# A first entry's attention in two ranges of nine tiles, products by 64 keys, and an order from measured durations

## The chip, the cores and the metric

One core of a Trainium2 chip. The metric is the device time of one execution in microseconds; lower is better.

## The reference

Inputs are q, k, v of shape (8, 8, 576, 64) (entries, heads, tokens, head size) and two matrices w_in (512, 2048) and w_out (2048, 512), all fp32.

```python
scores = 0.125 * q @ k^T                   # per entry and head
allowed: 0 <= i - j < 32                   # heads 0 to 3
         0 <= i - j < 128, (i - j) % 4 == 0   # heads 4 to 7
attn = exp(scores - max) ; attn /= sum + 1e-9
x = (attn @ v), heads side by side         # (4608, 512)
h = x @ w_in ; out = (h * sigmoid(1.702 h)) @ w_out
```

The dilated heads are stored with their tokens sorted by remainder of 4, so that both kinds of head are a band of 32 positions.

## The kernel before

**Layout.** A pair is two heads of one entry: 32 pairs, four to an entry, two of them plain and two dilated. x is kept transposed, 512 features in four chunks of 128, and a pair fills one chunk. The first three entries are multiplied in the plain way (`Group`, hidden chunks f = 0 to 15, up and down projection); the other five and the leftover 64 tokens of every entry go in three blocks through products of sums of matrices (`Block`). The fp32 numbers of the projections are split into a high and a low fp32r part, and one product is three matmuls of 128x512 (high x high, low x high, high x low). Attention itself is in fp32; one of its matmuls is two passes in the trace.

**The weights** come as 64-bit numbers, 32 units (`wi0`, `wo0`, `wi1`, ...) of 128x512. `decode` makes the high and low part of each from eight steps: load into one of five cells, value and low word on ACT (L393, L394), the sign on ACT or DVE (L387, L389), a shift on DVE, a sum, a copy as high part, a subtraction as low part (L348, on DVE or POOL). Hidden chunk f needs `wi{f}` and then `wo{f}`.

**Attention of a pair** (`scores`, `softmax`, `product` or, for the first entry, `first_product`, then `drain_x`). A tile is 32 queries by 64 keys. For the first entry the 576 queries are four ranges of 144 in the four groups of 32 partitions, five tiles to a range and head, of which the last is half empty: 640 columns for two heads. A bias matmul writes the mask first (L470), the scores are added (L482), then maximum, difference, exponential, sum, sum + 1e-9, reciprocal, two multiplications (one half each, usually on POOL), two 32x32 transposes. `first_product` (L572) multiplies into four PSUM banks, one a range, and waits for all four (`FOUR`). Its drain is a high part on ACT and a low part on DVE, from PSUM to `xh` and `xl` in the tile `xs`. For later pairs the transposed attention is copied into `bt` (64 keys by 32 queries for each window), and `product` (L595) is nine windows x two ranges x two heads = 36 matmuls of 32 columns with stationary v of 64x64.

**The order.** `Plan` collects all operations with costs by engine, urgency and dependences; `ordered` places them one after the other on a modelled time line and writes them out in that order for each engine, so an engine executes strictly what the list says. Where TensorE would be idle in the first 60 us it inserts matmuls on `ident` (L1243) or small ones (L1247). Its numbers decide order only.

Of the kernel before, what the change touches and what calls it, by code (L numbers as in the profile page):

```python
# [27 lines left out]
AHEAD = 0.58  # L28
# [7 lines left out]
NW = 9  # L36
HALF = 32 * NW
ROW = S // 4
INNER = 24


PE, ACT, DVE, POOL, DMA = range(5)
LATER = {PE: 0.0, ACT: 0.0, DVE: 0.51, POOL: 0.04, DMA: 0.0}
LATENCY = {PE: 0.3, ACT: 0.2, DVE: 0.2, POOL: 0.2, DMA: 0.2}


class Plan:

# [5 lines left out]

# [14 lines left out]

# [20 lines left out]
    def ordered(self, warm, warm_until, soon):  # L103
        order, starts = self.placed(warm_until, soon)
        for _ in range(ROUNDS):
            order, starts = self.placed(warm_until, soon, self.latest(starts, SINCE))
        ops = self.ops
        return [(ops[i][2] if i is not None and i >= 0 else lambda e, i=i: warm(i), e) for i, e in order]

    def placed(self, warm_until, soon, late=None):  # L110


# [8 lines left out]
        free = [0.0] * 5  # L121
        port, bus = [0.0], [0.0]
        issued, blocks = [0], [0.0]

        def start(i, e):
            held = port[0] if e == POOL or (e == DVE and ops[i][0][e] < 0) else 0.0
            if e == DMA and ops[i][1][0] >= 2000.0 and ops[i][0][e] > 100:
                held = bus[0] - 3.0
            if e == DMA and late is not None and SINCE < ready[i][e] < late[i] - CALM and late[i] < 9.0e3:
                held = max(held, ready[i][e] + 1.2)  # L130
            return max(free[e], ready[i][e], held)

        def fetched(count, when, cost):

            n = issued[0]
            issued[0] += count
            for j in range(len(blocks) - 1, 1 << 30):
                edge = 193 + 256 * j
                if edge >= n + count or edge > 1500:
                    return when + cost  # L140
                part = cost * (edge - n) / count
                at = max(when + part, blocks[j])
                blocks.append(at + (6.1 if at < 18.0 else 4.2))
                when, cost, n, count = at, cost - part, edge, count - (edge - n)
# [7 lines left out]
        while any(open_):  # L152
# [29 lines left out]
            if e == PE and when < warm_until:  # L182

                at, size = max(free[e], 1.0), 0.26 if when > 8.0 else 0.44
                if when < SHORT and blocks[-1] < when - 0.3:

                    small = min((193 + 256 * (len(blocks) - 1) - issued[0]) // 4 + 1, int((when - at - 0.1) / 0.045))
                    order.extend([(None, e)] * small)
                    at = fetched(4 * small, at, small * 0.045)
# [3 lines left out]
            order.append((i, e))  # L193
            starts[i] = when
            if e == PE:
                cost = fetched(ops[i][5], when, cost) - when
            if e == POOL or (e == DVE and ops[i][0][e] < 0):
                port[0] = when + cost

            free[e] = when + (cost if e != DMA else 0.7 if cost < 100 else 0.43)  # L200
            if e == DMA:
                bus[0] = max(bus[0], when + 2.0) + cost / 360.0
                cost = bus[0] - when
            for j in users[i]:
                for to in ready[j]:
                    gap = 0.0 if to == e == PE else 0.13 if to == e else LATENCY[to]
                    ready[j][to] = max(ready[j][to], when + cost + gap + ops[j][4])
# [4 lines left out]
        return order, starts  # L212
# [3 lines left out]
def tile_windowed_attention_then_gated_mlp(  # L216
# [3 lines left out]
    vp: bass.AP,  # L220
    first_v: bass.AP,
# [13 lines left out]
    plan = Plan()  # L235
# [16 lines left out]
    wi_last = temp([P, NF - NSUM, 2, DM], F32R, "wi_last", "wi_last")  # L252
    wo_kept = fixed([P, NOUT, 2, DM], F32R, "wo_kept")
    wo_last = temp([P, NF - NOUT, 2, DM], F32R, "wo_last", "wo_last")
# [5 lines left out]

    bt = fixed([P, 2, 2, NW + 1, 32], F32, "bt")
    bt_all = bt.rearrange("p y a n w -> p (y a n w)")
    arena = fixed([P, NU, GT], F32, "arena")
# [3 lines left out]

    def wi(f):
        return wi_kept[:, f] if f < NSUM else wi_last[:, f - NSUM]

    def wo(f):
        return wo_kept[:, f] if f < NOUT else wo_last[:, f - NOUT]
# [10 lines left out]
    prs = [fixed([P, 2, QT, W], F32, f"pr{j}") for j in range(2)]  # L283
    mxs = [fixed([P, 2, QT], F32, f"mx{j}") for j in range(3)]
    sms = [fixed([P, 2, QT], F32, f"sm{j}") for j in range(3)]
# [4 lines left out]
    prs.append(third[:, 0:2 * QT * W].rearrange("p (a t w) -> p a t w", a=2, t=QT))  # L290
    cts.append(third[:, 2 * QT * W:4 * QT * W].rearrange("p (h a t q) -> p h a t q", h=2, a=2, t=QT))
# [13 lines left out]
    ones = fixed([P, 32], F32, "ones")  # L305
    V.memset(ones, 1.0)
# [7 lines left out]
    early = arena[:, 17]  # L314
    classes = early.bitcast(BF16)[:, 0:QT * W].rearrange("p (t w) -> p t w", t=QT)
    band = early.bitcast(BF16)[0:32, QT * W:QT * W + W]
# [5 lines left out]
    for j in range(4):  # L322
        V.tensor_copy(out=plain[32 * j:32 * j + 32], in_=band[:, None, :].broadcast_to([32, QT, W]))

    A.activation(classes, plain, AF.Copy)
    V.memset(classes[:, 0, 0:32], NEG)
    V.memset(plain[0:32, 0, 0:32], NEG)

    def mask_dilated():

        A.activation(mask, plain, AF.Copy)
# [966 lines left out]
```

## Time and profile before

| | us |
|---|---|
| median of 3 runs | 836.37 (835.21 to 836.68) |
| profiled execution | 835.02 |
| its span | 833.2 |
| PE busy in the span | 816.0 (98%) |
| DVE, ACT, POOL busy | 641.1, 519.3, 331.3 |
| granted TensorE clock, mean | 0.994 |

PE is TensorE, DVE VectorE, ACT ScalarE, POOL GpSimd, SP the queue that issues loads and stores. Busy time of PE counts matmuls that overlap their neighbours, so what matters there is where it is idle and how far apart matmuls start. Idle time of another engine costs nothing unless PE waits for it.

### The profile page before, as it was taken

Reading aid. Unit: us, or ns where it says so; the run is one execution under the profiler, and the core shown is the slowest. Engines: PE = TensorE matmul, PEld = TensorE weight load, DVE = VectorE, ACT = ScalarE, POOL = GpSimd, SP = SyncE. Lnnn points to the kernel's source line nnn. Section 1 sums busy time; section 2 is a strip of 40 time slices with the busy share of each in tenths; the row PEclk is TensorE's granted clock in tenths of the full one; section 3 lists DMA queues with packets and bytes.
Section 4 is the critical chain, followed back from the end, with each engine's and each line's share of the span. In section 5 each row is a group of like instructions: output and inputs, shape, how many; then the busy total and the mean of one; then the engine's idle time right before and its main releaser. Section 6 shows DMA issues by size and latency. Waiting matters only on the chain.

```text
span 833.2 us, 20312 instructions
## 1 busy us (share of the span) xinstructions
PE 816.0 (98%) x8024; PEld 661.3 (79%) x8024; DVE 641.1 (77%) x1041; ACT 519.3 (62%) x964; POOL 331.3 (40%) x299
## 2 busy tenths in 40 slices
PE   6899999999999999999999999999999999999998
PEld 4678878888887888877878877888888888888886
DVE  6897898788897878887988899856468956465566
ACT  7898896776586667677666665445436534544430
POOL 3344326465545355233364454441223615204230
PEclk9799999999999999999999999999999999999999
DMA  9476867898887655997677969676556667655635
GB/s 358 148 256 184 246 193 228 305 299 281 298 279 261 234 188 195 344 320 237 215 263 237 290 217 284 230 256 212 183 184 203 201 215 262 206 190 193 199 124 180
DMA packets 110894, 195.70 MB, mean 235 GB/s; under 512 B 27728, under 2 KB 56656, under 8 KB 110800
## 3 DMA queue, kind: packets, MB, share of 16 engines
q1 hardware_dynamic: 110656, 194.29, 70.5%
q8 instruction: 63, 1.03, 0.5%
q14 instruction: 31, 0.25, 0.1%
q10 hardware_dynamic: 144, 0.13, 0.0%
HBM read 147.98 MB, written 45.09 MB: 232 GB/s over the span
## 4 chain that ended last, share of the span: by engine, by line
PE 90%; DVE 5%; issue 1%; DMA 1%; ACT 1%; SPq 0%; DVEq 0%; ACTq 0%
PE hp_m L850 16%; PE up_r L993 9%; PE up_q L993 8%; PE up_p L993 8%; PE second_q_Q L1111 5%; PE acc_m L787 5%; PE second_r_Q L1111 5%; PE acc_m L788 5%; PE acc_m L791 5%; PE second_p_Q L1111 4%; PE av L595 3%; PE sp L482 3%; PE second_r_Z L1111 3%; PE second_R L1111 3%; PE second_q_Z L1111 3%; PE second_p_Z L1111 2%
## 5 line engine op out<-in xcount | busy, mean ns | idle before, releaser
L348 POOL TENSOR_TENSOR arena<-arena 128x256 f32<-128x256 f32 (+3 forms) x112 | 120.0, 1084 | 155.0 <-DVE arena L348 53.5
L850 PE MATMUL hp_m<-xs,wi_kept 128*128 128x512 f32 x504 | 130.1, 400 | 0.6 <-DVE xs L348 0.4
L850 PEld LDWEIGHTS hp_m<-xs,wi_kept 128*128 128x128 f32 x504 | 93.5, 189 | 21.7 <-DVE xs L348 0.9
L993 PE MATMUL up_r<-wi_kept,xs 128*128 128x512 f32 x336 | 88.7, 389 | 0.0
L993 PE MATMUL up_q<-wi_kept,xs 128*128 128x512 f32 x336 | 87.5, 389 | 0.5 <-DVE arena L348 0.5
L993 PE MATMUL up_p<-wi_kept,xs 128*128 128x512 f32 x336 | 84.8, 395 | 0.8 <-ACT arena L341 0.6
L348 DVE TENSOR_TENSOR wo_kept<-arena,wo_kept 128x512 fp32r<-128x512 f32 x89 | 71.3, 811 | 18.1 <-ACT wo_kept L341 17.7
L341 ACT ACTIVATE wo_kept<-arena 128x512 fp32r<-128x512 f32 x104 | 64.4, 627 | 33.4 <-PE second_r_Q L1111 8.7
L348 POOL TENSOR_TENSOR wo_kept<-arena,wo_kept 128x512 fp32r<-128x512 f32 x32 | 43.1, 1350 | 97.0 <-ACT wo_kept L341 86.4
L993 PEld LDWEIGHTS up_p<-wi_kept,xs 128*128 128x128 f32 x336 | 61.8, 188 | 16.4 <-ACT arena L341 1.6
L993 PEld LDWEIGHTS up_q<-wi_kept,xs 128*128 128x128 f32 x336 | 63.0, 188 | 13.9 <-DVE arena L348 0.9
L993 PEld LDWEIGHTS up_r<-wi_kept,xs 128*128 128x128 f32 x336 | 63.1, 188 | 13.1
L348 POOL TENSOR_TENSOR pr<-pr,sm 128x320 f32<-128x320 f32 x52 | 42.2, 829 | 62.2 <-DVE sm L512 50.5
L348 POOL TENSOR_TENSOR wo_kept<-wi_last_units,wo_kept 128x512 fp32r<-128x512 f32 x20 | 28.6, 1428 | 83.7 <-ACT wo_kept L341 58.0
L787 PE MATMUL acc_m<-gh,wo_kept 128*128 128x512 f32 x156 | 61.5, 394 | 0.0
L788 PE MATMUL acc_m<-gh,wo_kept 128*128 128x512 f32 x156 | 60.8, 390 | 0.0
L341 ACT ACTIVATE bt<-ct 32x320 f32<-32x320 f32 x121 | 56.8, 469 | 4.7 <-DVE ct L533 2.5
L348 DVE TENSOR_TENSOR gl<-arena,gh 128x512 fp32r<-128x512 f32 x47 | 41.2, 877 | 11.8 <-PE acc_m L791 5.8
L348 DVE TENSOR_TENSOR arena<-arena 128x512 f32<-128x512 f32 (+1 forms) x63 | 47.2, 757 | 3.9 <-ACT arena L1015 1.7
L1015 ACT ACTIVATE arena<-arena 128x512 f32<-128x512 f32 x40 | 25.1, 627 | 35.1 <-DVE arena L348 35.0
L341 ACT ACTIVATE wo_kept<-wi_last_units 128x512 fp32r<-128x512 f32 x46 | 28.8, 629 | 25.9 <-PE second_r_Z L1111 7.1
L858 ACT ACTIVATE arena<-hp_m 128x512 f32<-128x512 f32 x48 | 28.6, 597 | 25.2 <-PE hp_m L850 16.1
(260 smaller groups left out, 1868.4 us busy)
## 6 DMA issues: line engine op xcount, KB each, us to landing
xs<-sums SPq DMA_DIRECT2D x168, 256.0 KB, 3.3
out_weights<-sums_o SPq DMA_DIRECT2D x63, 512.0 KB, 3.9
qk<-qk_dram SPq DMA_DIRECT2D x29, 576.0 KB, 5.6
v<-vp_dram SPq DMA_DIRECT2D x28, 576.0 KB, 4.4
xs<-sums_o SPq DMA_DIRECT2D x21, 512.0 KB, 3.5
sums<-arena SPq DMA_DIRECT2D x32, 256.0 KB, 4.3
sums_o<-arena SPq DMA_DIRECT2D x32, 256.0 KB, 4.7
arena<-wi_dram SPq DMA_DIRECT2D x15, 512.0 KB, 4.7
```

The costliest lines, as they stand in the source:

```text
L341: A.activation(dst, src, AF.Copy, scale=scale)
L348: (V if e == DVE else G).tensor_tensor(out=dst, in0=a, in1=b, op=op)
L482: T.matmul(dst[:, w:w + n], u["qk"][rows, at:at + 32], u["qk"][rows, S + first:S + first + n], start=not masked(k), stop=True, tile_positi ...
L595: T.matmul(to[rows, 0:32], u["v"][keys, a, m], bt[keys, k % 2, a, m], start=True, stop=True, tile_position=(D * r, D * a), skip_group_chec ...
L787: T.matmul(self.acc[j], w[:, 0, cols], high, start=f == 0, stop=False)
L788: T.matmul(self.acc[j], w[:, 1, cols], high, start=False, stop=False)
L791: T.matmul(self.acc[j], w[:, 0, P * j:P * j + P], low, start=False, stop=f == NF - 1)
L850: T.matmul(hps[f], wi(f)[:, st, cols], mv[:, c], start=c == 0 and k == 0, stop=c == NC - 1 and k == 2)
L858: add({ACT: 0.60}, -10.0, lambda e: A.activation(g32, hps[f], AF.Tanh, scale=0.851), (place,), ("g32",))
L993: T.matmul(self.banks[place], xs[:, slot, at:at + P], wi_kept[:, 2 * a + c, mv], start=fresh and c == 0 and k == 0, stop=c == 1 and k == 2 ...
L1015: add({ACT: 0.60}, -10.0, lambda e: A.activation(unit(dst), src(), AF.Gelu_apprx_sigmoid), need, keys)
L1111: T.matmul(self.second[key], w[:, st, cols], mv, start=fresh and y == 0 and k == 0, stop=y == 1 and k == 2, skip_group_check=True)
```

## The change

**First entry.** Two ranges of 288 queries, nine tiles each; the four groups of 32 partitions are range and head, so a pair has 9 x 64 = 576 columns and 36 score matmuls, without the key ranges cut at the end. The masks of single tiles come from five bands (`first_masks`), by matmuls of 64 to 448 columns. The 1e-9 is a 65th column of each tile and goes into the sum, so the small addition is gone for all pairs. `first_product` uses two of the four banks, in turn; for the first two pairs (plain heads) v is loaded with zeros in the other head's 64 columns, so that one matmul of 64 keys and 128 columns serves both heads (19 instead of 46 matmuls); the dilated ones keep 64 columns (36 instead of 40). The inputs of the first entry go where the last weights will be decoded (`wo_last`, `wi_last`, the arena, the `qk` tile) and no weight's cell is taken from other tiles any more.

**Later pairs.** v is cut in blocks of 64 keys, six and four to the two ranges, 768 columns instead of 1152; a block meets 96 queries, so `bt` holds 64 keys by 96 queries with zeros in the corners (cleared once), and `product` is 20 blocks, two of them cut at a bank's end: 22 matmuls of 32 to 96 columns that add up in PSUM. Drains are cut accordingly.

**Order.** The planner has other costs, a model of late instruction blocks, of landing loads and of a lowered clock, and takes the best of its four rounds.

```diff
-NW = 9
-HALF = 32 * NW
+LOW = 8
+SPAN = W + 32
+NT = S // 64
+WIDE_QK, WIDE_V = (2, 2, 2, 2), (P, P, D, D)
+FIRST_QK, FIRST_V = (-9.0, -8.04, -4.96, -4.2), (-8.44, -6.17, -3.7, -3.23)
+EARLY = {0: 1.63, 1: 12.3, 2: 14.6, 3: 16.9}
+FIRST_W = {0: -8.22, 1: -7.65, 2: -5.03, 3: -4.69, 4: -2.5}
...
-    bt = fixed([P, 2, 2, NW + 1, 32], F32, "bt")
+    bt = fixed([P, 2, 2, QT, SPAN], F32, "bt")
...
-    ones = fixed([P, 32], F32, "ones")
-    V.memset(ones, 1.0)
+    ones = ident.bitcast(F32)[:, 0:32]
...
+    G.memset(bt[:, :, :, :, 0:W], 0.0)
...
+    def first_masks(k):
+        u = pairs[k]
+        sp = bank([P, 2, GT], "sp", f"sp_{k}").rearrange("p a n -> p (a n)")
+        u["all"] = sp[:, 0:NT * W].rearrange("p (t w) -> p t w", w=W)
+        spans = ((0, 1, 2), (1, 4, 0), (4, 5, 3), (5, 6, 4), (6, 8, 0), (8, 9, 0)) if dilated(k) else (
+            (0, 1, 1), (1, 8, 0), (8, 9, 0))
+        for t, to, n in spans:
+            T.matmul(sp[:, W * t:W * to], ident, bands[:, n:n + 1].broadcast_to([P, to - t, W]), start=t in (0, 8),
+                     stop=False, skip_group_check=True)
+
+    def first_scores(k):
...
+        for t in range(NT):
+            for r in range(2):
+                i = NT * r + t
+                keys = slice(at + 32 * i - 32, at + 32 * i + 32)
...
+                for a in range(2):
+                    rows, g = slice(D * a, D * a + D), 2 * r + a
+                    T.matmul(u["all"][32 * g:32 * g + 32, t], u["qk"][rows, 32 * i:32 * i + 32], u["qk"][rows, keys],
+                             start=False, stop=True, tile_position=(D * a, 32 * g), skip_group_check=True)
...
-    def inverse(k, urgency):
-        sm, SM = sms[turn(k)], f"sm{turn(k)}"
-        add({DVE: -0.15}, urgency, lambda e: V.tensor_scalar(
-            out=sm, in0=sm, scalar1=1.0e-9, scalar2=None, op0=ALU.add), (), (SM,))
...
+    def first_banks(k):
+        return f"acc{2 * (k % 2)}", f"acc{2 * (k % 2) + 1}"
...
+        for s in range(0 if dilated(k) else -1, NT):
+            for r in range(2):
+                if s < 0 and r == 0:
                     continue
...
+                for a in range(P // WIDE_V[k]):
+                    rows = slice(D * r, D * r + D) if WIDE_V[k] == P else slice(D * r + 32 * a, D * r + 32 * a + 32)
+                    T.matmul(u["x"][WIDE_V[k] * a:WIDE_V[k] * a + WIDE_V[k], r, at:at + n], u["v"][rows, s % (NT + 1)],
+                             ct[rows, first:first + n], start=begin, stop=s == NT - 1,
+                             tile_position=(rows.start, WIDE_V[k] * a), skip_group_check=True)
...
-        for m in range(NW):
+        pieces = [(r, a, m) for m in range(QT + 1) for r in range(2) for a in range(2) if r or 0 < m < QT]
+        begun = set()
+        for r, a, m in pieces:
+            rows, keys = slice(D * a, D * a + D), slice(D * r, D * r + D)
+            first, last, at = max(SPAN * m - W, 0), min(32 + SPAN * m, SPAN * QT if r else SPAN * QT - SPAN), max(W * m - W, 0)
...
+            for n, (to, at, first, last) in enumerate(parts):
+                if first < last:
+                    T.matmul(to[rows, at:at + last - first], u["v"][keys, a, m], bt_flat[keys, k % 2, a, first:last],
+                             start=(r, a, n) not in begun, stop=True, tile_position=(D * r, D * a), skip_group_check=True)
+                    begun.add((r, a, n))
```

How the order moves, at three places. On PE, before, the fourth pair's scores (`sp`) and the second pair's product (`first_x`) at 19 to 26 us stand like this:

```order
L482 MATMUL sp_439<-arena 32x64 x35
L482 MATMUL sp_439<-arena 32x48
L482 MATMUL sp_439<-arena 32x16
L482 MATMUL sp_439<-arena 32x64 x3
L572 MATMUL first_x<-ct_92,arena 64x32 x6
L572 MATMUL first_x<-ct_92,arena 64x64 x24
L572 MATMUL first_x<-ct_92,arena 64x48 x8
L572 MATMUL first_x<-ct_92,arena 64x16 x8
L850 MATMUL hp_m_0_556<-xs,wi_kept 128x512 x3
```

and now, the third pair's scores (`sp_312`) with the products of the first (`ct_84`) and second pair (`ct_85`), then masks and scores of the fourth (`sp_419`):

```order
L658 MATMUL first_x<-ct_84,first_135 128x64 x16
L658 MATMUL first_x<-ct_84,first_135 128x32 x2
L537 MATMUL sp_312<-arena 32x64 x36
L953 MATMUL hp_m_0_391<-xs,wi_kept 128x512 x3
L658 MATMUL first_x<-ct_85,arena 128x32
L658 MATMUL first_x<-ct_85,arena 128x64 x16
L658 MATMUL first_x<-ct_85,arena 128x32 x2
...
L517 MATMUL sp_419<-arena,ident 128x128
...
L537 MATMUL sp_419<-arena 32x64 x36
```

The second product has moved ahead of the fourth scores, and both are shorter.

On ACT, before, the last two drains (`xs<-first_x 128x4x128`) and the steps up to the first chunk's tanh (`hp_m_0`):

```order
L341 ACTIVATE xs<-first_x 128x4x128
L393 ACTIVATE arena<-arena 128x512 x2
L394 ACTIVATE arena<-arena 128x512 x2
L387 ACTIVATE arena<-arena 128x512
L341 ACTIVATE xs<-first_x 128x4x128
L394 ACTIVATE arena<-arena 128x512
L387 ACTIVATE arena<-arena 128x512
L393 ACTIVATE arena<-arena 128x512
L858 ACTIVATE arena<-hp_m_0_556 128x512
```

and now, from the six decoding steps ahead of the fourth exponential (`pr_82`) to the fourth drain (L432 is the value, L433 the low word, L426 the sign):

```order
L433 ACTIVATE arena<-arena 128x512
L426 ACTIVATE arena<-arena 128x512
L592 ACTIVATE pr_82<-pr_82 128x9x64
L383 ACTIVATE xs<-first_x 128x4x128
L383 ACTIVATE wo_kept<-arena 128x512
L433 ACTIVATE arena<-arena 128x512
L426 ACTIVATE arena<-arena 128x512
L432 ACTIVATE arena<-arena 128x512
L433 ACTIVATE arena<-arena 128x512
L432 ACTIVATE arena<-arena 128x512
L433 ACTIVATE arena<-arena 128x512
L383 ACTIVATE xs<-first_x 128x4x128
```

Seven steps stand between the last two drains instead of five, and the fourth exponential is right ahead of the third drain.

On SP, before, the first loads (`wi_dram` and `wo_dram` are weights):

```order
L427 DMA qk_126<-qk_dram 128x1152
L383 DMA arena<-wi_dram 128x512
L440 DMA v_129<-first_v_dram 128x768
L427 DMA arena<-qk_dram 128x1152
L383 DMA arena<-wo_dram 128x512
L427 DMA arena<-qk_dram 128x1152
L383 DMA arena<-wi_dram 128x512
L383 DMA bt<-wo_dram 128x512
L427 DMA arena<-qk_dram 128x1152
L440 DMA arena<-first_v_dram 128x768
```

and now (a weight is 524 KB, a load of 1152 columns 590 KB, one of 1280 columns 655 KB):

```order
L473 DMA first_135<-first_qk_dram 128x1152
L487 DMA first_135<-first_v_dram 128x1280
L422 DMA arena<-wi_dram 128x512
L473 DMA first_qk_139<-first_qk_dram 128x1152
L422 DMA arena<-wo_dram 128x512
L487 DMA arena<-first_v_dram 128x1280
L473 DMA arena<-first_qk_dram 128x1152 x2
L487 DMA first_v_199<-first_v_dram 128x576
L487 DMA arena<-first_v_dram 128x576
L422 DMA arena<-wi_dram 128x512
```

All inputs of the first entry now stand ahead of the third weight, where four weights stand between them in the rows of before.

## Rows read from the trace of the kernel before

**Rows 1.** Stretches: length, busy PE, PEld, DVE, ACT, POOL (instructions), granted clock, DMA, GB/s

```profile
0.00:20.00 20.00, 13.62 (x478) 8.49 (x479) 12.86 (x35) 15.30 (x22) 6.78 (x15) 1.00 0.91 356
20.00:25.00 5.00, 2.48 (x128) 2.25 (x127) 4.60 (x10) 4.88 (x7) 2.85 (x3) 0.63 0.49 188
...
40.00:130.00 90.00, 89.77 (x1064) 72.00 (x1063) 78.70 (x141) 80.93 (x141) 35.30 (x30) 1.00 0.69 217
42.00:829.00 787.00, 783.51 (x7174) 639.23 (x7172) 609.21 (x969) 484.67 (x914) 317.26 (x277) 1.00 0.71 234
```

**Rows 2.** Waits of PE: total us, times, longest

```profile
PE sp L482 <- issue: 3.8, 3, 2.0
...
PE first_x L572 <- issue: 1.2, 1, 1.2
```

**Rows 3.** Timeline of PE: start, length, line, shape, count, idle before

```profile
4.86 1.45 PE L482 MATMUL sp<-qk 64*32 64x64 f32 x84
...
15.27 0.38 PE L482 MATMUL sp<-arena 64*32 64x64 f32 x21 [1.67 <-issue]
15.58 1.50 PE L572 MATMUL first_x<-ct,v 32*64 32x32 f32 x92
...
19.28 0.32 PE L482 MATMUL sp<-arena 64*32 64x64 f32 x9
21.56 1.37 PE L482 MATMUL sp<-arena 64*32 64x64 f32 x75 [1.96 <-issue]
22.85 1.18 PE L572 MATMUL first_x<-ct,arena 32*64 32x32 f32 x53
25.21 0.91 PE L572 MATMUL first_x<-ct,arena 32*64 32x64 f32 x39 [1.18 <-issue]
...
34.29 1.08 PE L572 MATMUL first_x<-ct,arena 32*64 32x64 f32 x80
...
38.46 3.93 PE L850 MATMUL hp_m<-xs,wi_kept 128*128 128x512 f32 x16 [0.42 <-DVE xs L348]
42.23 0.39 PE L787 MATMUL acc_m<-gh,wo_kept 128*128 128x512 f32 x1
```

**Rows 4.** Timeline of ACT, DVE and POOL, first 46 us

```profile
5.64 0.67 ACT L393 ACTIVATE arena<-arena 128x512 f32<-128x512 f32 x1 [0.39 <-DMA arena<-wi_dram]
...
6.68 0.81 DVE L502 TENSOR_REDUCE mx<-sp 128x10 f32<-128x640 f32 x1
...
6.90 1.34 ACT L387 ACTIVATE arena<-arena 128x512 f16<-128x512 f32 x1
...
8.39 0.74 ACT L506 ACTIVATE pr<-pr 128x640 f32<-128x640 f32 x1
...
10.50 0.17 DVE L510 TENSOR_SCALAR sm<-sm 128x10 f32<-128x10 f32 x1
...
11.66 1.58 POOL L348 TENSOR_TENSOR pr<-pr,sm 128x320 f32<-128x320 f32 x2 [6.70 <-DVE sm L512]
...
35.41 1.08 ACT L341 ACTIVATE xs<-first_x 128x512 fp32r<-128x512 f32 x1 [0.49 <-PE first_x L572]
...
37.33 1.08 DVE L348 TENSOR_TENSOR xs<-first_x,xs 128x512 fp32r<-128x512 f32 x1
```

**Rows 5.** Timeline of all engines near 99 us

```profile
98.51 1.29 POOL L348 TENSOR_TENSOR wi_kept<-arena,wi_kept 128x512 fp32r<-128x512 f32 x1 [3.63 <-ACT wi_kept L341]
...
99.78 2.88 PE L850 MATMUL hp_m<-xs,wi_kept 128*128 128x512 f32 x12
```

**Rows 6.** Timeline of PE around one product and one scores

```profile
102.59 0.25 PE L595 MATMUL av<-bt,v 64*64 64x32 f32 x2
...
103.77 0.50 PE L787 MATMUL acc_m<-gh,wo_kept 128*128 128x512 f32 x1
...
108.07 0.97 PE L482 MATMUL sp<-qk 64*32 64x64 f32 x72
108.97 1.65 PE L850 MATMUL hp_m<-xs,wi_kept 128*128 128x512 f32 x6
```

More of the change, by code (lines that the diff above doesn't have):

```diff
@@ L27 @@
 NU = 22
-AHEAD = 0.58
+AHEAD = 0.62
 ROUNDS, SINCE, CALM, ROOM = 3, 130.0, 8.0, 2.5
@@ L103, in ordered @@
     def ordered(self, warm, warm_until, soon):
-        order, starts = self.placed(warm_until, soon)
-        for _ in range(ROUNDS):
-            order, starts = self.placed(warm_until, soon, self.latest(starts, SINCE))
+        best = None
+        late = None
+        for n in range(ROUNDS + 1):
+            order, starts, end = self.placed(warm_until, soon, late)
+            if best is None or end < best[1]:
+                best = order, end
+            late = self.latest(starts, SINCE)
+        self.ends.append(best[1])
         ops = self.ops
-        return [(ops[i][2] if i is not None and i >= 0 else lambda e, i=i: warm(i), e) for i, e in order]
+        return [(ops[i][2] if i is not None and i >= 0 else lambda e, i=i: warm(i), e) for i, e in best[0]]
+    ends = []
     def placed(self, warm_until, soon, late=None):
@@ L136, in fetched @@
             issued[0] += count
[L137 to L144, printed above, removed]
+            recent.append((n, when))
+            while True:
+                k = len(arrived) - 1
+                edge = FIRST_EDGE + BLOCK * k
+                if edge >= n + count:
+                    break
+                part = cost * max(0.0, edge - n) / count
+                at = max(when + part, arrived[k])
+                ahead = [t for m, t in recent if m >= edge - DECODED]
+                asked = max(arrived[k], min([at, *ahead]))
+                arrived.append(asked + (6.2 if asked < 18.0 else 4.4 if bus[0] > asked + 0.3 else 3.0))
+                when += at - when - part
+            del recent[:-60]
+            return when + cost
         open_ = [set() for _ in free]
@@ L211, in placed @@
                         open_[to].add(j)
-        return order, starts
+        return order, starts, free[PE]
 @with_exitstack
@@ L610, in drain_x @@
         if k >= INNER:
+            near = [(0, low, lambda first, last: u["x"][:, 0, first:last], True)]
+            far = (lambda first, last: u["x"][:, 1, first - low:last - low]), True
+        else:
+            near = [(0, ROOMY, lambda first, last: u["x"][:, 0, QT * W + first:QT * W + last], True),
+                    (ROOMY, low, lambda first, last: u["x"][:, 1, QT * W + first - ROOMY:QT * W + last - ROOMY], True)]
+            far = (lambda first, last: u["av"][:, first - low:last - low]), False
@@ L726, in attention @@
         places = ("sp",) if k >= INNER else ("left", "av", "sp") if joint else ("left", "av")
-        add({PE: 1.8 if joint else 0.85}, urgency - 1.0e5, work,
-            (lots(k)[1], *(f"bt{k % 2}.{m}" for m in range(8)), *need), places, 1.0)
+        add({PE: 2.26 if joint else 1.35}, urgency - 1.0e5, work,
+            (lots(k)[1], *(f"bt{k % 2}.{m}" for m in range(8)), *need), places, 0.0, count=234 if joint else 90)
         if joint:
```

512 lines of the change are left out of this document (296 added, 216 removed).

## The prediction, made before the changed kernel was run

> **What bounds the kernel now.** I read the stretches first [rows 1]. From 42 to 829 us TensorE is busy 783.51 of 787 us, so once it runs densely only 3.5 us are idle: there the time is the sum of TensorE's own instructions. The first 40 us are different: 2.48 of 5 us busy between 20 and 25, at a granted clock of 0.63. So the change can act in two ways: bring the dense stretch forward, or change what TensorE itself has to do in it. Other engines count only where TensorE waits for them.
>
> Next the waits of TensorE [rows 2]: the largest is "issue", time in which it waited for nothing that the profile shows, 3.8 us before scores and 1.2 us before the first entry's products. The timeline gives the places [rows 3]: 1.67 us before 15.27, 1.96 before 21.56, 1.18 before 25.21. Counting weight loads and matmuls as two instructions, between the first two stand 21 and 9 score matmuls, 92 of the product, three idle and two mask matmuls: 2x127 = 254; between the last two 75 + 53 matmuls: 256. So a block of about 256 instructions came late each time, and I number the edges 702, 956 and 1212 from the start. The Trainium skill (Runtime: NRT & Kernel Launch, Instruction fetch mechanics) says that blocks are 256 instructions and that crossing one is mostly hidden. This trace agrees on the size and not on the hiding; by that sentence the second step below would bring nothing, about 0.9 us less.
>
> Last, what ends the start: the fourth pair's product begins at 34.29, its drain runs on ScalarE from 35.41 and on VectorE from 37.33 [rows 4], and TensorE is dense from 38.46 with 16 of the 36 matmuls of the first three hidden chunks still to do; the second projection follows at 42.23 [rows 3].
>
> **The start, step by step.** (1) Loads. v of the first pair is 655 KB instead of 393 and now stands ahead of the first weight, which lands later by 655 KB at 356 GB/s [rows 1], 1.8 us after 5.64 [rows 4]. ScalarE takes two steps of that weight (0.67 each) ahead of the first exponential, so this starts at about 8.8 to 9.3 instead of 8.39. The first product still comes earlier, near 13.7 instead of 15.58, because the second pair's sum no longer stands ahead of its second transpose. None of this reaches the end by itself.
>
> (2) Instructions. Scores have 36 matmuls instead of 42, the first two products 19 instead of 46, each two passes of two instructions, so up to edge 956 the new program has all of the first two products and three quarters of the fourth scores behind it, where the old one had just begun them. If the block comes when it did, the fourth scores end near 22.0, not 22.85. Nothing excludes that it comes up to 1 us later, since the small first matmuls now wait for the identity.
>
> (3) The softmax of the third and fourth pairs. Rows are 576 wide instead of 640, so 0.81 us becomes 0.73 and 1.58 about 1.45; one small operation (0.17) goes [rows 4]. The third pair: scores done near 16.8 (edge 702 at 15.27, then a third of them); maximum behind the second pair's transposes to 18.35; difference 19.05; exponential (0.74) 19.8; sum 20.55; two low parts of the second drain 21.2; reciprocal 21.4; GpSimd's two products 23.0; transposes 23.35. The fourth pair's maximum is queued behind those transposes: 24.1, difference 24.8. Its exponential is queued on ScalarE behind six steps of two weights (order of ScalarE above). Ahead of those weights 5.3 MB are loaded, 15 us at 356 GB/s, so the first lands near 19.5; four steps of 0.6 and two of 1.3 from 20.9 end at 25.7, and the exponential at 26.4. Sum 27.1, reciprocal 27.3, GpSimd 28.85, transposes 29.3: the fourth product starts at about 29.4, 4.9 us sooner than 34.29. One reason is that a product now needs two banks and not all four, so it no longer waits for the previous drain.
>
> (4) The last drain. Between the third and fourth drains ScalarE has seven decoding steps, 1.27 + 6 x 0.57 = 4.7 us after 27.4 (lengths of [rows 4] less the tenth by which one overlaps the next), so the fourth drain starts near 32.0 though its product is done near 30.7. It takes 1.08, the low part on VectorE 1.08 [rows 4]: dense from 34.2 instead of 38.46, with 18 matmuls left instead of 16 (0.23 each by 12 from 99.78 to 102.59 [rows 5, 6]): 3.8 us gained. Then tanh, gate and high part of the first chunk, with two decoding steps more on ScalarE, let the second projection begin about 0.7 us after TensorE is ready for it. **Start: -3.1 us.** Bounds: -5.4, if the decoding steps on ScalarE (1.3 before the drain, 1.0 before the exponential) do not get in the way; +0.9, if the clock is at its half level (1.2 GHz) when the dense stretch begins, which makes 18 matmuls 0.45 us each, +4. It was lowered from 20 to 25 us before (0.63 [rows 1]) and back by 38.46, where 16 matmuls take 3.77 us [rows 3].
>
> **The dense stretch.** 28 products lie in it. One now takes 103.77 - 102.59 = 1.18 us [rows 6]: 36 matmuls, 72 passes of 32 columns, on two row groups side by side, 29.2 ns for a pass in its group. The new one has 22 matmuls, 44 passes; its longer group has 24, sixteen of 96 columns, four of 32, four of 64. From below: 29.2 ns a pass whatever its length, 0.70 us against 1.05, -0.35 each. From above: columns set the pace, 0.91 ns each, sixteen of 87.5 ns: 1.75 us, +0.70 each. The nearest row is the scores': 72 passes of 64 columns in 0.90 us [rows 6], 25 ns in a row group, so length alone does not set the pace. At 0.44 ns a column (0.23 us for 512) without overlap, or 0.91 with full overlap, sixteen take 43 ns each, 0.91 us, -0.14 each; with the two passes of a matmul one after the other and a 29 ns step between matmuls, 54.5 ns, +0.10. I take -0.05, **-1.4 us** in all, with -9.8 and +19.6 as ends. The Trainium skill (TensorEngine Tiling (Array Packing), Instruction Overhead) says that a matmul costs about 60 cycles however few its columns. By it, 32 columns cost as much as 60, 96 cost 1.6 times that, the group takes 0.94 of what it did, and the sum would be -1.7; the 29.2 ns row fits it roughly.
>
> Scores (36 matmuls both times), the 128x512 matmuls and the second masks cost what they did. The removed small operations, the smaller loads of v (197 KB less, 28 times), the transposes, copies and extra drain pieces lie on VectorE, ScalarE and the queue beside dense TensorE work: 78.70 and 80.93 of 90 us busy from 40 to 130 us [rows 1]. Cover is thin there (rival 1); later it is ample. The new costs in the planner reorder everything after 130 us, where at most a share of 3.5 us can be won; I take 0.
>
> **Sum.** -3.1 - 1.4 = -4.5 us. The profiled execution took 835.02 (span 833.2 and 1.8 around it), so 830.5; the median of the runs is 1.35 above it, so 831.9.
>
> **Rivals.** (1) The weights become late instead. They are decoded just in time: the low half of one ends at 99.80 where its matmul starts at 99.78 within the rows' rounding [rows 5]. With the dense stretch 3 to 4 us earlier, ScalarE has the same 80.93 us of work in 86. If the decoding does not move forward, the whole start gain is given back as waits between 50 and 125 us: only -1.4 stays, 835.0. For it speaks that two thirds of the start saving come from work and not from waiting less; against it that VectorE and GpSimd (35.30 of 90) have room and that the new order puts more there. 0.15.
> (2) Slower: columns set the pace of the products. Place: the 28 products; price up to +0.70 each, with the start -3.1 + 19.6 = +16.5, 852.9. It decides from +0.11 each, a 96-column pass of about 55 ns or more; every 10 ns above are 0.19 us each and 5 in all. Against it the scores' row; for it that no row has a product with more than 64 columns on halves of the array. 0.12.
> (3) The change does not do what it says at the start: blocks come late by the new counts, or the clock is low, and the dense stretch starts as before. -3.1 + 4.0 - 1.4: 835.9. 0.05.
> (4) More: products at the floor of 29.2 ns, -9.8 - 3.1, 823.5. 0.08.
>
> **How the numbers follow.** The forecast has 0.60: 831.9, its own range 827.5 to 835 from the start's bounds and -0.14 to +0.10 a product. Two runs of this kernel can be told apart from about 0.2%, 1.7 us. Of rivals 1 and 3 most is "same", of 2 most "slower". Faster 0.72, same 0.14, slower 0.14. Range 826.5 to 838.5: it leaves out the far ends of 2 and 4.
>
> **What would show it.** Dense TensorE from 33 to 36 us with the second projection at 37 to 39; the fourth scores ending by 22 to 23; the fourth product near 29.5 and its drain on ScalarE right behind decoding steps; a product of 1.0 to 1.3 us from its first matmul to the next 128x512; idle from 42 to the end under 5 us. Wrong if products take over 1.3 us, if waits on low halves of weights show between 50 and 125 us, or if the block edges stall later than before.

## The result, and the profile after

The changed kernel takes 827.83 us (median of five runs, 826.59 to 829.07), the kernel before 836.68 beside it (835.21 to 837.78): a ratio of 0.9895, 95% interval 0.9878 to 0.9913. The forecast was 831.9 in a range of 826.5 to 838.5. So the sign and the range hold, and the gain is about twice the 4.5 us forecast. A second set of six runs (first experiment below) gave 829.74 against 836.6, ratio 0.9914 (0.9891 to 0.9937), one and a half times the forecast.

The profiled execution took 829.07 with a span of 827.3. The stretches, as in [rows 1] (length, busy PE, PEld, DVE, ACT, POOL, granted clock, DMA, GB/s):

```profile
0.00:20.00 20.00, 14.59 (x389) 10.58 (x390) 11.35 (x32) 8.99 (x16) 11.70 (x27) 1.00 0.83 320
20.00:25.00 5.00, 4.22 (x113) 3.54 (x111) 3.50 (x8) 3.80 (x8) 1.30 (x2) 1.00 0.13 39
...
40.00:130.00 90.00, 86.42 (x932) 68.08 (x931) 78.18 (x143) 76.34 (x138) 20.20 (x19) 1.00 0.67 215
42.00:829.00 787.00, 776.71 (x6353) 634.68 (x6351) 605.07 (x940) 482.38 (x954) 316.00 (x274) 1.00 0.69 229
```

Between 20 and 25 us TensorE is busy 4.22 us instead of 2.48, at a clock of 1.00 instead of 0.63. Between 40 and 130 it now idles 3.6 us, where it idled 0.2. (The last row includes 5.8 us behind the last matmul.) The timeline of TensorE in the start, against [rows 3]:

```profile
10.14 1.21 PE L537 MATMUL sp<-first_qk 64*32 64x64 f32 x72 [1.25 <-DMA first_qk<-first_qk_dram]
...
14.28 0.43 PE L517 MATMUL sp<-arena,ident 128*128 128x64 bf16 x6 [1.32 <-DVE pr L390]
14.64 2.41 PE L658 MATMUL first_x<-ct,first 64*128 64x32 f32 x38
16.99 1.21 PE L537 MATMUL sp<-arena 64*32 64x64 f32 x72
...
19.45 2.39 PE L658 MATMUL first_x<-ct,arena 64*128 64x32 f32 x38
...
22.12 1.21 PE L537 MATMUL sp<-arena 64*32 64x64 f32 x72
...
31.50 1.29 PE L658 MATMUL first_x<-ct,arena 32*64 32x64 f32 x72
...
35.92 2.66 PE L953 MATMUL hp_m<-xs,wi_kept 128*128 128x512 f32 x10 [0.47 <-DVE xs L390]
38.90 0.50 PE L890 MATMUL acc_m<-gh,wo_kept 128*128 128x512 f32 x1 [0.32 <-ACT gh L383]
```

No wait of the start is "issue" any more. The fourth product starts at 31.50 instead of 34.29, the second projection at 38.90 instead of 42.23, but with 6 of the 36 matmuls still to do (30 stand in the trace up to there, 36 before): 1.36 us, so the start is worth 42.23 - 38.90 - 1.36 = 1.97 us. A product, as in [rows 6], from its first matmul to the 128x512 matmul behind it:

```profile
77.98 0.25 PE L684 MATMUL av<-bt,v 64*64 64x32 f32 x2
...
78.23 0.25 PE L684 MATMUL av<-bt,v 64*64 64x96 f32 x2
78.29 0.25 PE L684 MATMUL sp<-bt,v 64*64 64x96 f32 x2
78.31 0.25 PE L684 MATMUL av<-bt,v 64*64 64x96 f32 x2
...
79.02 0.97 PE L953 MATMUL hp_m<-xs,wi_kept 128*128 128x512 f32 x3
```

79.02 - 77.98 = 1.04 us instead of 1.18; the scores still take 0.90. The waits of TensorE that came into the dense stretch (`gh` is the high part of a gated hidden chunk, `out_weights` a load for the blocks, `pr` and `bt` belong to the attention of a later pair), out of the list that [rows 2] is from (total, times, longest):

```profile
PE second_p_Q L1214 <- DMA out_weights<-sums_o: 1.3, 1, 1.3
...
PE acc_m L890 <- ACT gh L383: 1.1, 2, 0.8
PE av L684 <- issue: 1.0, 1, 1.0
...
PE sp L547 <- DVE pr L390: 0.8, 1, 0.8
```

**Where the time went.** The last matmuls of TensorE begin at 826.87 before and 821.01 after; in the second profile of the changed kernel (first experiment) at 818.33. The three profiles give this account; waits are the idle stretches over 0.1 us behind the second projection's start, added up:

| us | before | after | after, second profile |
|---|---|---|---|
| start: second projection, less matmuls left | 42.23 | 40.26 | 40.37 |
| its gain | | 1.97 | 1.86 |
| 28 products, 1.18 to 1.04 | | 3.92 | 3.92 |
| waits behind it | 3.45 | 5.02 | 2.50 |
| their gain | | -1.57 | 0.95 |
| rest | | 1.54 | 1.81 |
| last matmuls begin earlier by | | 5.86 | 8.54 |

The rest is in no single wait. Counted from each matmul's start to the next one's, less the waits, it lies for the most part in the 128x512 matmuls: the 1008 of `up`, the blocks' up projection, take 232.2 us before and 230.7 and 230.5 after, and those of `hp_m` 0.4 less for the same number. Why these steps are shorter is open. In the same count the 28 products together gain 3.4 us and not 3.9: 24 of them take 1.04 us in the changed kernel, the other four 1.21 to 1.54.

### The profile page after: what moved, and what is told of

The parts are those of the page before. It is cut to its first block, busy times and chain, and to the rows that moved or that the text cites. A ratio compares the mean times of both kernels' runs of the same rounds, so it can differ in the third digit from the quotient of the medians.

```text
span 827.3 us, 18378 instructions
## 1 busy us (share of the span) xinstructions
PE 810.0 (98%) x7040; PEld 658.1 (80%) x7040; DVE 635.3 (77%) x1005; ACT 510.5 (62%) x1000; POOL 337.1 (41%) x310
## 4 chain that ended last, share of the span: by engine, by line
PE 88%; DMA 4%; DVE 4%; ACT 2%; issue 1%; SPq 0%; POOL 0%; DVEq 0%; ACTq 0%; POOLq 0%
PE hp_m L953 13%; PE up_r L1096 9%; PE up_q L1096 9%; PE up_p L1096 9%; PE second_p_Q L1214 5%; PE second_q_Q L1214 5%; PE second_r_Q L1214 5%; PE acc_m L890 5%; PE acc_m L894 4%; PE acc_m L891 4%; PE sp L559 3%; PE second_p_Z L1214 3%; PE second_R L1214 3%; PE second_r_Z L1214 3%; PE second_q_Z L1214 3%; PE av L684 2%
## 5 line engine op out<-in xcount | busy, mean ns | idle before, releaser
L390 POOL TENSOR_TENSOR arena<-arena 128x256 f32<-128x256 f32 (+4 forms) x114 | 120.4, 1065 | 121.0 <-DVE arena L390 27.3
L390 POOL TENSOR_TENSOR wo_kept<-arena,wo_kept 128x512 fp32r<-128x512 f32 x43 | 59.7, 1391 | 124.2 <-ACT wo_kept L383 91.2
L390 DVE TENSOR_TENSOR wo_kept<-arena,wo_kept 128x512 fp32r<-128x512 f32 x78 | 62.9, 814 | 15.4 <-ACT wo_kept L383 14.6
L1096 PEld LDWEIGHTS up_p<-wi_kept,xs 128*128 128x128 f32 x336 | 62.4, 188 | 13.7 <-DVE arena L1121 0.3
L390 POOL TENSOR_TENSOR pr<-pr,stats 128x320 f32<-128x320 f32 (+1 forms) x52 | 40.8, 802 | 73.3 <-DVE stats L603 72.1
L390 DVE TENSOR_TENSOR arena<-arena 128x512 f32<-128x512 f32 (+2 forms) x77 | 63.2, 825 | 2.6 <-ACT arena L1118 0.8
L383 ACT ACTIVATE bt<-ct 32x256 f32<-32x256 f32 (+1 forms) x128 | 56.7, 443 | 4.4 <-DVE ct L617 2.2
L390 DVE TENSOR_TENSOR gl<-arena,gh 128x512 fp32r<-128x512 f32 x51 | 44.2, 867 | 8.0 <-PE acc_m L894 4.1
L383 ACT ACTIVATE gh<-arena 128x512 fp32r<-128x512 f32 x59 | 37.4, 635 | 15.2 <-DVE arena L962 6.8
L962 DVE SCALAR_TENSOR_TENSOR arena<-arena,hp_m 128x512 f32<-128x512 f32 x48 | 32.8, 684 | 16.2 <-ACT arena L961 15.8
```

The source lines that it names most:

```text
L383: A.activation(dst, src, AF.Copy, scale=scale)
L390: (V if e == DVE else G).tensor_tensor(out=dst, in0=a, in1=b, op=op)
L962: add({DVE: 0.69}, -10.0, lambda e: V.scalar_tensor_tensor(out=g32, in0=g32, scalar=1.0, in1=hps[f], op0=ALU.add, op1=ALU.mult), (place,), ...
L1096: T.matmul(self.banks[place], xs[:, slot, at:at + P], wi_kept[:, 2 * a + c, mv], start=fresh and c == 0 and k == 0, stop=c == 1 and k == 2 ...
```

## The experiments

**1. Both kernels again.** No edit.

> The changed kernel once more, nothing edited. Theory A, the step from the kernel before to it is about 9 us and the profiled execution of it was a slow one: 826 to 828.5 us, with no wait for instruction blocks and a granted clock of 1.00 in the first 40 us, and idle time of TensorE behind 40 us under the 5.3 us of the first profile. Theory B, the medians shown first were a lucky set: 829 to 831 us, that is the 6 us that the two profiled executions differ by.

> The kernel before once more, for a second profile. Theory A, its profiled execution was a fast one by chance of the start: now a span of 834 to 838 us, with the waits for instruction blocks and the granted clock between 20 and 35 us as before or worse. Theory B, it differs behind 42 us: idle time there 4.5 us or more instead of 3.5, with the start the same within 0.3 us.

The changed kernel: 829.74 us (826.36 to 831.02), ratio 0.9914 (0.9891 to 0.9937); the profiled execution took 826.36. The start agrees to about 0.1 us, and the dense stretch idles less:

```profile
40.00:130.00 90.00, 87.63 (x1006) 69.37 (x1006) 79.73 (x147) 77.07 (x139) 21.58 (x20) 1.00 0.66 215
42.00:829.00 787.00, 776.57 (x6353) 634.65 (x6352) 604.36 (x940) 482.73 (x954) 315.63 (x274) 1.00 0.70 229
```

The waits for `out_weights` (1.33), `pr` (0.78) and `bt` (0.47) are gone; what stays is 0.58 at 41.35, 0.78 for `gh` and 1.01 "issue" near 115 us. So those three waits stand in one execution and not in another of the same program. The profile is as theory A had it, the median as theory B. The kernel before took 835.11, span 832.6, with the start as in [rows 3] within 0.1 us and 3.27 us of idle behind it. Both theories on it fall, since its profile repeats. This run was on another chip, where the median of the kernel before is 834.31 (832.14 to 837.99), so this time the profiled execution was slower than the median. The gain is 6.0 and 8.7 us between profiled executions and 6.9 to 8.9 between medians.

**2. The order of a product's pieces.** Three kernels change this one line, and with it no other instruction's place:

```diff
-pieces = [(r, a, m) for m in range(QT + 1) for r in range(2) for a in range(2) if r or 0 < m < QT]
+pieces = [(r, a, m) for a in range(2) for m in range(QT + 1) for r in range(2) if r or 0 < m < QT]
+pieces = [(r, a, m) for r in range(2) for m in range(QT + 1) for a in range(2) if r or 0 < m < QT]
+pieces = [(r, a ^ r, m) for m in range(QT + 1) for a in range(2) for r in range(2) if r or 0 < m < QT]
```

r is the range (keys 0 to 63 or 64 to 127 of the array's rows), a the head (which half of the columns). The first puts the heads apart, the second the ranges apart, the third takes the four quarters in another turn.

> The changed kernel with the 22 matmuls of a later pair's product in another order: all blocks of the first head, then all of the second, so that the two column halves of the array are never used in neighbouring matmuls of one row group. Theory: the two halves do not overlap, a pass of 96 columns takes its row group 42 ns whatever stands beside it; a product stays at 1.04 us (1.0 to 1.1) and the kernel within 1 us. Rival: a pass takes 85 ns and neighbours in the other half hide half of it; then a product takes 1.6 to 1.9 us and the kernel 16 to 24 us more.

> The changed kernel with a product's matmuls in another order: all blocks of the first range (upper rows of the array), then all of the second (lower rows). Theory: the two row groups stream side by side and matmuls start in program order, so apart they add up: 0.75 and 0.91 us instead of 1.04 together, 1.6 to 1.8 us a product, 15 to 21 us more for the kernel. Rival: the array takes the next matmuls of a free row group from further ahead in the program; then a product stays near 1.04 to 1.2 and the kernel within 4 us.

> The changed kernel with the pieces of a product ordered so that two neighbours differ in key range and in head each time where they can (range 0 head 0, range 1 head 1, range 0 head 1, range 1 head 0); so every second step stays on the same half of the columns. Theory A, only the alternation of column halves lets passes overlap: a product gets slower, 1.2 to 1.45 us against 1.04, and the time 4 to 11 us longer, 832 to 839 us. Theory B, any change of row group does as well: 0.95 to 1.1 us a product, 825 to 830 us.

Heads apart: 848.2 us, ratio 1.0136 (1.0097 to 1.0175), a product 1.70 us: the theory set down for it falls and its rival holds. Ranges apart: 841.43, ratio 1.0055 (1.0028 to 1.0082), nearly every product 1.43 to 1.60, between the theory's 1.6 to 1.8 and the rival's 1.04 to 1.2. Another turn: 829.32, ratio 0.9926 (0.9898 to 0.9954), a product 1.04, as in the changed kernel. With the heads apart the trace shows why:

```profile
77.57 0.24 PE L684 MATMUL av<-bt,v 64*64 64x96 f32 x1
77.62 0.24 PE L684 MATMUL sp<-bt,v 64*64 64x96 f32 x1
77.65 0.24 PE L684 MATMUL av<-bt,v 64*64 64x96 f32 x1
...
77.73 0.24 PE L684 MATMUL av<-bt,v 64*64 64x96 f32 x1
...
79.02 0.73 PE L953 MATMUL hp_m<-xs,wi_kept 128*128 128x512 f32 x2
```

In a range (`av` is the second, `sp` the first) a 96-column pass follows the last after 80 ns in both kernels, but here each step holds one pass and in the changed kernel two, one for each head (x2 at 78.23, 78.31). In the kernel before, 18 steps of two 32-column passes fill 1.05 us of the 1.18, 58 ns each:

```profile
102.72 0.23 PE L595 MATMUL av<-bt,v 64*64 64x32 f32 x2
...
102.78 0.23 PE L595 MATMUL av<-bt,v 64*64 64x32 f32 x2
...
102.84 0.23 PE L595 MATMUL av<-bt,v 64*64 64x32 f32 x2
```

So a quarter of the array paces its own passes by length, about 58 ns for 32 columns and 80 for 96, and the four quarters run side by side if the code takes them in turn: 24 ns a pass over all (1.04 us for 44), against 39 with two quarters in turn. A rival, that passes overlap only if every change of quarter changes the column half as well, falls with the third kernel: there every second change stays in one half, and a product still takes 1.04 us. 28 x 0.66 us is 18.5; 848.2 is 18.5 above the second set's 829.74 and 20.4 above the first set's 827.83. The Trainium skill (TensorEngine Tiling (Array Packing), Tiling Modes) says that tiles work independently and in parallel; the trace agrees, with 24 ns a pass over four quarters against 39 over two.

**3. Wide v.** The first edit takes the 128-column v away from both of the first pairs, the second from the second pair.

```diff
-WIDE_QK, WIDE_V = (2, 2, 2, 2), (P, P, D, D)
+WIDE_QK, WIDE_V = (2, 2, 2, 2), (D, D, D, D)
+WIDE_QK, WIDE_V = (2, 2, 2, 2), (P, D, D, D)
```

> The changed kernel with v of the first two pairs kept at 64 columns instead of 128 padded with zeros: their products are 38 matmuls of 64 columns of v instead of 19 of 128, and 330 KB less are loaded for each. Theory A: the wide products are slow by themselves (2.4 us each in the trace after, against 1.0 to 1.5 for the old ones) and lie on the way to the fourth product, so narrow ones take 1.2 to 1.5 us, the fourth product starts 1 to 2 us sooner than 31.5, and the kernel takes 1 to 2 us less. Theory B: the blocks of instructions decide; with about 130 instructions more up to the fourth scores, waits called issue come back (1 to 2 us each) and the kernel takes 1 to 3 us more.

> The changed kernel with v of 128 columns for the first pair alone; the second pair has 76 matmuls of 64 columns instead of 38 of 128 and loads half as much. Theory A, a wide product is slow (2.4 us against 1.35 for the narrow one), and it pays only because of the instruction blocks: the second product 1 us shorter, its 152 more instructions bring a wait for a block of 0.5 to 2 us back, second projection at 39 to 41.5 us, 827 to 831 us. Theory B, the wide products are needed for both pairs: blocks late and clock low as with none wide, second projection past 43 us, 833 to 836 us.

None wide: 835.75 us, ratio 0.9995 (0.9979 to 1.001). One wide: 837.24, ratio 1.0008 (0.9993 to 1.0023). Both lose all that the change had won, and the first shows "issue" waits of 0.45 and 1.92 us in the start, a clock of 0.68 and 0.64 between 20 and 30 us, and the second projection at 44.76. That looked like the instruction blocks. But both edits also change the planner's counts and load costs, so the order is another, and the one wide kernel has its second projection at 39.71 and 10.9 us of idle behind 38 us. So the same edits were made once more, with the planner left with the old counts and costs; the order is then that of the changed kernel:

```diff
+PLAN_V = (P, P, D, D)
-add({DMA: 5 * WIDE_V[k] if k < NC else 390}, ...
+add({DMA: 5 * PLAN_V[k] if k < NC else 390}, ...
-first_banks(k), count=(72 if dilated(k) else 76) * P // WIDE_V[k])
+first_banks(k), count=(72 if dilated(k) else 76) * P // PLAN_V[k])
```

> The changed kernel with no wide v (76 matmuls of 64 columns for each of the first two pairs, as in the run without wide v), but the planner is still given the counts and load costs of the wide ones, so that the order of the changed kernel stays. Theory A, the instruction blocks alone cost what that run lost: the first two products 1.35 us instead of 2.4, then waits for blocks of 2 to 4 us between 15 and 26 us and a clock under 1.00 behind them, dense TensorE 2 to 4 us later, 830 to 834 us. Theory B, that run lost by its new order behind 40 us: here 826 to 830 us, with 9 to 10 us of idle time gone again behind 40 us.

> The changed kernel with wide v for the first pair alone, and the planner still given the counts and load costs of two wide ones, so that the order stays. Theory A, the 11 us that the same edit lost with a new order are the order's: here 826 to 831 us, second projection at 38.5 to 40.5 us, idle time of TensorE behind 40 us under 6 us. Theory B, they are the blocks': waits for blocks of 2 us or more before 35 us and 833 to 838 us again.

None wide, order held: 829.7 us, ratio 0.9939 (0.9919 to 0.996). One wide, order held: 829.69, ratio 0.9942 (0.9921 to 0.9963). Neither can be told from the changed kernel's 0.9914; the first set's 0.9895 is lower by 0.0045, which is 3.8 us, while the times lie at most 1.9 us apart. These two were timed on the other chip too, so whether wide v is worth a few us is not decided. The start with none wide:

```profile
13.04 1.35 PE L658 MATMUL first_x<-ct,first 32*64 32x32 f32 x76
...
15.54 1.09 PE L537 MATMUL sp<-arena 64*32 64x64 f32 x63 [0.85 <-issue]
...
20.57 0.43 PE L658 MATMUL first_x<-ct,arena 32*64 32x64 f32 x14 [1.97 <-issue]
...
38.30 0.49 PE L890 MATMUL acc_m<-gh,wo_kept 128*128 128x512 f32 x1 [0.30 <-ACT gh L383]
```

The blocks are late again, by 0.85 and 1.97 us, and yet the second projection comes 0.6 us earlier than with wide v: the second pair's scores start at 9.41 instead of 10.14, behind a smaller load of v, and each of the first two products takes 1.35 us instead of 2.4. The clock stays at 1.00. A third late block follows, 1.34 us at 68 us. With one wide no block is late, and the second projection comes at 39.50, 0.6 us later than with two. So the theory that the blocks decide falls: of what the same edits lost before, 5 to 8 us (0.9995 - 0.9939 and 1.0008 - 0.9942 by the ratios, 6.1 and 7.6 us by the times) were the order's.

**4. The order alone.** The new planner in the kernel before (its operations, counts and costs stay), and the changed kernel with one number of the planner changed:

```diff
-AHEAD = 0.58
+AHEAD = 0.62
...
+BLOCK, FIRST_EDGE, DECODED = 256, 195, 38
...
-EXACT, MARGIN = 42.1, 1.148
+EXACT, MARGIN = 42.1, 1.0
```

> The kernel before with the planner's new model of time alone (late blocks, landing loads, lowered clock, best of four rounds); its attention, its loads and the costs of its operations stay. Theory A, the order is worth nothing: 834.5 to 838 us, products at 1.18 us, second projection at 41.5 to 43 us. Theory B, the order brings the start by itself: second projection at 39 to 41 us and 832 to 834.5 us. Theory C, the order fits only the new operations: more waits between 40 and 130 us, 838 to 842 us.

> The changed kernel with another order and nothing else: the planner's costs behind 42 us are taken as they are instead of 1.148 times. Theory A, the order behind the start is worth several us: idle time of TensorE behind 40 us 8 to 12 us instead of 2.8 to 5.3, a lowered clock in one stretch, 831 to 838 us. Theory B, any sensible order does: 826 to 831 us.

The new planner on the old operations: 837.51 us, ratio 1.0012 (0.9997 to 1.0027); "issue" waits of 0.43, 1.49 and 1.62 us in the start, a clock of 0.50 (the lower level, 1.2 GHz) from 25 to 35, the second projection at 47.60. It brings nothing by itself. The other order: 850.2 us, ratio 1.019 (1.0165 to 1.0216), with a start like the changed kernel's (second projection at 38.72). Its waits:

```profile
PE hp_m L953 <- DVE arena L962: 6.0, 6, 2.2
PE av L684 <- DMA bt<-ct: 2.9, 2, 1.7
PE second_R L1214 <- DVE arena L390: 1.6, 2, 0.8
```

Idle behind 38 us is 16.0 instead of 5.3, and the granted clock 0.83 from 60 to 70 and from 170 to 180 us. The profiled executions differ by 20.6 us. Waits make up half of it. The other half lies in the steps between the 128x512 matmuls of the three entries that are multiplied in the plain way: from start to start, less the waits, `hp_m` and `acc_m` take 272.8 us instead of 261.5, some 4 us of it in the two stretches with the lowered clock, the rest spread. Behind the last matmul nothing is lost (3.6 us to the end of the span, 4.1 in the changed kernel). Theory A was right in kind and far too small.

**5. Decoding behind the softmax.** The value, low word and sign steps of the second hidden chunk's weights (n = 2 and 3) have to wait for the fourth exponential, those of the third chunk's (4 and 5) for the high part of the fourth drain.

```diff
+behind = ("pr1",) if n in (2, 3) else ("xh3.0",) if n in (4, 5) else ()
-A.activation(value, f32(at["top"]), AF.Copy, scale=2.0 ** -112), (R,), (E,))
+A.activation(value, f32(at["top"]), AF.Copy, scale=2.0 ** -112), (R, *behind), (E,))
...
-add({DVE: -0.75, ACT: 1.37}, urgency, take_sign, (R,), (R + "l",))
+add({DVE: -0.75, ACT: 1.37}, urgency, take_sign, (R, *behind), (R + "l",))
```

> The changed kernel, with one thing added to the order: ScalarE's value, low-word and sign steps of the second weights (wi1, wo1) may only stand behind the fourth pair's exponential, those of the third weights (wi2, wo2) only behind the fourth pair's drain. Theory (the fourth step of the prediction): these steps delay the fourth exponential and the fourth drain, so without them the fourth drain begins 1.5 to 2.5 us sooner than 33.5 us, TensorE is dense from about 33.5 to 34.5 instead of 35.9, and the kernel takes 1 to 2 us less. Rival: the weights are needed anyway and now come later; TensorE then waits for them between 35 and 60 us and the kernel takes the same or up to 2 us more.

835.21 us, ratio 0.998 (0.9962 to 0.9997). The fourth exponential did not come earlier but at 28.20 instead of 27.16, with ScalarE idle for 4.36 us ahead of it. Part of this is the clock, 0.72 from 15 to 20 us, which made the third scores 2.03 us long instead of 1.21. The second projection starts at 39.98 with 12 matmuls left, 2.4 us later than in the changed kernel, and then waits of 1.09 and 1.46 us at 62 and 65 are followed by a lower clock:

```profile
65.00:70.00 5.00, 3.54 (x51) 2.28 (x50) 4.56 (x10) 4.18 (x9) 1.26 (x2) 0.84 0.65 173
70.00:75.00 5.00, 5.00 (x88) 3.79 (x88) 2.94 (x5) 3.99 (x6) 2.63 (x4) 0.81 1.03 413
```

The fourth exponential then waited for its own difference on VectorE, not for decoding, so taking these steps out of its way did not bring it forward. The edit moved the order as well, so it does not price the steps alone.

None of these kernels is faster than the changed one beyond the noise.

## Why the prediction was right, and where it was off

**The products** were the term that was mis-sized: -0.05 us each was taken, -1.4 in all, and -0.14 each was measured, -3.9 (-3.4 with the four slower ones counted as they are). The value -0.14 stood among the cases ("0.91 with full overlap"), and the second experiment shows that it is the true one: the passes of the two heads run side by side. The step that failed is the reading of a pass in its row group as 29.2 ns: it was two passes in 58 ns on two halves of the columns. Rival 2, columns set the pace with 0.91 ns each, comes near when that overlap is taken away: 1.70 us a product, where its bound was 1.18 + 0.70; but columns alone do not set the pace even there, as 32 take 58 ns and 96 take 80. By an estimate from the sentence of the Trainium skill on overhead (TensorEngine Tiling (Array Packing), Instruction Overhead), 96 columns would cost 1.6 times what 32 do; the steps of 80 and 58 ns make it 1.4, and the gain was larger than the -1.7 it led to.

**The start** gave 1.9 to 2.0 us instead of 3.1. No block is late, as forecast, and yet all is 0.5 to 1.3 us later: first exponential at 9.79 (8.8 to 9.3 forecast), first product at 14.64 (13.7), fourth scores done at 23.3 (22.0). Two steps failed. Step (1) did not count that the larger v delays the second pair's load too: its scores wait 1.25 us for it, and the third pair's mask, which stands ahead of the first product, 1.32 us for their difference (rows at 10.14 and 14.28 above). And step (3) gave the first product no length of its own. It takes 2.41 us, its drain runs behind it, and on VectorE the drain stands ahead of the second pair's transposes and so of the third pair's maximum (VectorE and ScalarE of the changed kernel):

```profile
17.79 0.46 DVE L390 TENSOR_TENSOR xs<-first_x,xs 128x288 fp32r<-128x288 f32 x1 [0.77 <-ACT xs L383]
...
18.84 0.83 DVE L610 STREAM_TRANSPOSE ct<-pr 128x320 f32<-128x320 f32 x2
19.60 0.72 DVE L588 TENSOR_REDUCE stats<-sp 128x9 f32<-128x576 f32 x1
20.35 0.76 DVE L390 TENSOR_TENSOR pr<-sp,stats 128x576 f32<-128x576 f32 x1
...
26.15 0.76 DVE L390 TENSOR_TENSOR pr<-sp,stats 128x576 f32<-128x576 f32 x1
...
27.16 0.73 ACT L592 ACTIVATE pr<-pr 128x576 f32<-128x576 f32 x1
...
33.53 1.09 ACT L383 ACTIVATE xs<-first_x 128x512 fp32r<-128x512 f32 x1
```

The differences of the third and fourth pair come at 20.35 and 26.15 where 19.05 and 24.8 were forecast, 1.3 late both. The six decoding steps ahead of the fourth exponential, which the working named as its cause, hold it by no more than 0.25 us (its difference on VectorE ends at 26.91, it starts at 27.16). The last drain starts 1.5 us late at 33.53, TensorE is dense from 35.92 instead of 34.2 with 16 matmuls left instead of 18. Experiment 3 bears it out: with the small v and the order held the second scores start at 9.41, the first product at 13.04 and takes 1.35 us, and the second projection comes 0.6 us earlier in spite of the blocks. So step (2), fewer instructions, did what it says, and the start did not need it.

**The dense stretch.** Idle from 42 to the last matmul is 4.5 us, under the 5 us named. But rival 1 came true in part: 3.4 us of new waits between 40 and 130 us, 2.1 in the second profile. None of them is for the low half of a weight; the one wait of that kind is in the start, 1.17 us before 29.37, ended by the subtraction on GpSimd. The largest that repeats is 1.0 us of "issue" near 115 us, of which the profile shows no cause, and next the cast `gh`, which stands on ScalarE behind a decoding step (ScalarE and TensorE of the changed kernel):

```profile
112.88 1.35 ACT L426 ACTIVATE arena<-arena 128x512 f16<-128x512 f32 x1
...
113.97 0.68 ACT L383 ACTIVATE gh<-arena 128x512 fp32r<-128x512 f32 x1
...
114.70 0.50 PE L890 MATMUL acc_m<-gh,wo_kept 128*128 128x512 f32 x1 [0.77 <-ACT gh L383]
```

**The order** was priced at 0 with the argument that at most a share of 3.5 us could be won. As a gain that is nearly right. As a loss it had no price at all, and experiment 4 shows one of 20 us or more: the range was safe only because this order happens to fit.

**From the profile to the median** the sum added 1.35 us. That step is no constant: the profiled execution was 0.8 us above the median in the second profile of the kernel before, and 1.2 above and 3.4 below it in the two of the changed kernel. So a microsecond or more of how near the forecast came is chance.

Rival 3 did not happen: no block was late in the start in either profile of the changed kernel, and the clock was 1.00 throughout its start. The "issue" near 115 us is no edge of a block either. It stands ahead of the same product, the fourth, behind 2905 instructions in both profiles and behind 3057 and 2981 in the two kernels with the order held, while edges are 256 apart. Of rival 4's 12.9 us, the products gave 3.9.

**Open** are why the steps of `up` and `hp_m` are shorter, and what the clock does in executions that were not profiled. That it does something the runs show: in 22 runs of the kernel before, beside the second set, the mean granted clock is 0.986 to 0.994 (median 0.991) and in its two profiled executions 0.994; in the eleven runs of the changed kernel it is 0.992 to 1.000. A lower clock goes with a longer time: of the ten runs of experiment 5 the one at 1.000 took 832.57 us, the one at 0.989 838.45. So a part of the gain in the medians may be a clock that falls less; where it falls in those runs is not on record.

## What to carry to other kernels

Read the overlap of small matmuls from how many passes start together in one step, not from passes divided by time; then longer passes can be priced by the step, and the code has to visit all quarters of the array in turn. Where a planner sets the order, an edit that changes a cost or a count is two edits: hold the order fixed to price the first, or a loss of 5 to 8 us is put down to the wrong cause. Trace each forecast of a chain through every engine's own queue, the short first links too: a load and a product of 2.4 us at the head of it moved everything behind them by 1.3.

## What the runs showed of the hardware that was not expected

Half as many matmuls can take longer: 38 passes of 64 rows by 128 columns took 2.41 us, 76 passes of 32 rows by 64 columns for the same product 1.35.

The granted clock differs between executions of the same instructions. With the ranges apart, whose first 40 us are those of the changed kernel, it fell between 15 and 20 us, and the second projection came at 40.62 instead of 38.90:

```profile
15.00:20.00 5.00, 5.00 (x112) 4.67 (x111) 3.25 (x9) 1.46 (x5) 4.34 (x6) 0.68 0.66 237
```

It did not fall in the start with none wide and the order held, where TensorE stood for 0.85 and then 1.97 us, and fell to 0.81 in experiment 5 behind waits of 1.09 and 1.46.
